# Polysketch attention and ReGLU FFN on one core: the first 512 tokens in feature layout, their queries loaded first, and a new order of all operations

## The chip, the core and the metric

The kernel runs on one core of one Trainium2 chip. The engines are written as in the profile: PE (TensorE; PEld is its weight load), DVE (VectorE), ACT (ScalarE), POOL (GpSimd) and SP (SyncE, which here issues transfers). The metric is the device time of one execution in microseconds (us), the median of several runs. The clock column of the profile is the share of the full TensorE clock that was granted.

## The reference, cut to what matters

```python
# q, k, v: (4 batches, 4 heads, 1088 tokens, 32), float32; S1, S2: (8, 32)
def phi(x):
    a = np.einsum('rd,bhsd->bhsr', S1, x)
    b = np.einsum('rd,bhsd->bhsr', S2, x)
    return np.einsum('bhsi,bhsj->bhsij', a, b).reshape(*x.shape[:-1], r * r)
q_p, k_p = (phi(q), phi(k))
kv = np.einsum('bhsf,bhsd->bhfd', k_p, v)
z = np.sum(k_p, axis=2)
num = np.einsum('bhsf,bhfd->bhsd', q_p, kv)
den = np.einsum('bhsf,bhf->bhs', q_p, z)[..., None] + 1e-06
x = num / den                       # laid out as 4352 tokens x 128
# w_gate, w_val: (128, 1536); w_out: (1536, 128)
gate = np.maximum(x @ w_gate, 0.0)
out = (gate * (x @ w_val)) @ w_out  # (4352, 128), float32
```

So each token's query and key are sketched twice to 8 numbers, the outer product gives 64 features, the keys of a batch are summed into a state of 64 x 32 (and a normaliser z of 64) for each head, every query is multiplied with its batch's state and divided by the normaliser, and the result goes through an FFN with a gate. No token needs another's result except through the states, so the FFN of a batch's tokens can run as soon as the keys of this batch, and these queries, are through.

## The kernel before

A `Plan` holds every operation (`Op`) with its engine and what it comes after. `START` gives each operation a rank; `Plan.run` sorts by rank and emits in that order, which is thus the order of each engine's queue. An engine takes its queue in order: an operation that waits holds up all behind it. `BANKS` gives each `Lease` its PSUM bank, and `WARM` says ahead of which operations dummy matmuls on a tile of zeros stand (L967). `POOL_UNITS` lists the FFN units whose product of gate and value is made by POOL.

The operations come in four families.

- `K(b)`, keys and values of batch b: transposes of the loaded keys on DVE (`kt1`, L467 and L471), the sketch on PE (`ksk`, L486, in runs of 8 x 32 columns for four groups of partitions, with the ninth tile of every group in matmuls of 32 columns of its own, half of them on a weight of zeros `wz`), a transpose back on DVE (`kt2`, L491), the normaliser (`z`, `zc`, then `w`, `wc`), the outer products (`kphi`, POOL or DVE, L527), casts of v to f16 on ACT (`vc`, and `vcr`, L548, for the ninth tile, which has loads of its own), the state on PE (`kv`, L554) and its copy into a block-diagonal tile `bd` (`kve`; L564 on ACT for batch 0, L566 on DVE for the others).
- `First`, the first two tiles (256 tokens) of batch 0, on a short way of their own: sketch (L630), transposes, the normaliser by `aT` and `csk` (L642, L648), then on DVE `f bw` (L654), `f red` (L610), `f rd` (L612); numerators on PE (`f num`, L677) with tokens on partitions; `f xd` (DVE, L615) multiplies by the reciprocal; a PE transpose (`f xr`, L684) and an ACT copy (`f x`, L621) give x with features on partitions, as the FFN wants it.
- `Q(b, ...)`, all other queries: `qt1` (DVE, L940), sketch `qsk` (PE, L748, L755), `qt2` (DVE, L761), `bw` (POOL, L769), `red` and `rd` (DVE, L775, L779), `an` and `qphi` (POOL, L783, L789), a transpose `qtr` (for the first tiles on PE, L804, else a DMA from the SP queue, L796), `num` (L816) and a copy `x` to the FFN's input (ACT, L829). `Q(0)` takes tiles 2 to 7 of batch 0, in parts of two and four.
- `F(u, group, ...)`, 102 FFN units of 512 columns of gate and of value: `g` and `v` (PE, L870), `relu` (ACT, L875), `h` (DVE, L883) or, for POOL's units, `vcp` (ACT, L879) and `hp` (POOL, L887), then `o` (PE, L894), which adds up over the units of a group in one PSUM bank; at its last unit `oe` (ACT, L902) and the stores. Groups are (0,0,2), (0,2,2), (0,4,4) for batch 0 as batch, first tile, number of tiles; two of four tiles for each later batch; and a last one of 256 tokens, the ninth tiles of all batches.

The loads: batch 0's keys, S1, S2, a first 256 columns of q (`q00`, 128 KB), half of v, and then the rest of q (`q01`, 416 KB) on SP; the other half of v and all nine weight blocks as casting transfers from POOL's queue. q has four buffers, k and v two each.

Of the kernel before, what the change touches and what calls it, by code (L numbers as in the profile page):

```python
# [9 lines left out]
FP32 = mybir.dt.float32  # L10
FP16 = mybir.dt.float16
# [12 lines left out]
POOL_UNITS = set(range(20, 96, 6))  # L24
START = [
# [48 lines left out]
]  # L74
BANKS = [
# [22 lines left out]
]  # L98
WARM = {33: 29, 62: 1, 64: 3, 152: 1, 66: 1, 79: 6, 80: 3, 81: 3, 83: 2, 158: 2, 266: 10}
# [39 lines left out]
def kernel(  # L139
# [53 lines left out]
    q_sb = [sb([128, NC * D], FP32, f"q_sb{b}") for b in range(B)]  # L193
    v32 = [sb([128, H, NX * D], FP32, f"v32_{b}") for b in range(2)]
    v32 = v32 + v32
    vr32 = sb([64, B, H, D], FP32, "vr32")
# [5 lines left out]
    kT = [sb([128, NC * 32], FP32, f"kT{b}") for b in range(2)]  # L202
# [5 lines left out]
    id16 = sb([2 * R, 2 * R], FP32, "id16")  # L208
# [4 lines left out]
    maskp = sb([128, 2], FP32, "maskp")  # L213
    maskh = sb([128, 4], FP32, "maskh")
    wS = sb([128, 2, 2, R], FP32, "wS")
    wz = sb([128, 32], FP32, "wz")
# [18 lines left out]

    def by_q(t, lo, hi):
        return t[:, lo // 2 * QY:hi // 2 * QY].rearrange("p (y a c) -> p a y c", a=4, c=64)

    def load_v0(eng, y, a):
        eng.dma_start(  # L240
            out=v32[0][32 * a:32 * a + 32, :, y * GX * D:(y + 1) * GX * D],
# [763 lines left out]
```

## Time and profile before

| what | value |
|---|---|
| runs | 105.74, 106.45, 107.58 us; median 106.45 |
| span of the profiled execution | 105.4 us |
| busy PE, DVE, ACT, POOL | 94.6, 84.8, 78.4, 62.5 us |
| instructions | 3159 |
| dummy matmuls (L967) | 61, 7.2 us |
| transferred | 11.87 MB |

The span of the profiled execution runs from its first instruction to its last; it lies 0.3 us under the fastest run and 1.05 under the median. A row of a group gives busy time, mean time of one in ns, and the idle time ahead of them with what ended it; a row of the chain gives start, length and what; a row of stretches gives the borders, the length, each engine's busy time, the granted clock, the share of the transfer engines and GB/s.

### The profile page before, as it was taken

Reading aid. Unit: us, or ns where it says so; the run is one execution under the profiler, and the core shown is the slowest. Engines: PE = TensorE matmul, PEld = TensorE weight load, DVE = VectorE, ACT = ScalarE, POOL = GpSimd, SP = SyncE. Lnnn points to the kernel's source line nnn. Section 1 sums busy time; section 2 is a strip of 40 time slices with the busy share of each in tenths; the row PEclk is TensorE's granted clock in tenths of the full one; section 3 lists DMA queues with packets and bytes.
Section 4 is the critical chain, followed back from the end, with each engine's and each line's share of the span. In section 5 each row is a group of like instructions: output and inputs, shape, how many; then the busy total and the mean of one; then the engine's idle time right before and its main releaser. Section 6 shows DMA issues by size and latency. Waiting matters only on the chain.

```text
span 105.4 us, 3159 instructions
## 1 busy us (share of the span) xinstructions
PE 94.6 (90%) x1239; PEld 65.9 (63%) x1239; DVE 84.8 (80%) x184; ACT 78.4 (74%) x160; POOL 62.5 (59%) x75
## 2 busy tenths in 40 slices
PE   6997249999999999999999989999999999999930
PEld 6777127578577666656665555667666666779910
DVE  4595297289999999999999978998997794978820
ACT  5207212769899779989979899897598999995820
POOL 6989129769238354999898499787540724404000
PEclk9999975599999999999999999999999999999995
DMA  2999999996000795700057610005293021221442
GB/s 57 272 183 285 279 277 256 221 236 165 8 0 3 142 301 146 176 9 0 0 99 231 126 61 0 6 0 109 50 126 102 24 48 51 42 101 62 100 96 57
DMA packets 15311, 11.87 MB, mean 113 GB/s; under 512 B 9408, under 2 KB 13376, under 8 KB 15296
## 3 DMA queue, kind: packets, MB, share of 16 engines
q1 hardware_dynamic: 13184, 10.04, 38.7%
q0 software_dynamic: 1872, 1.31, 8.5%
q10 hardware_dynamic: 240, 0.33, 1.1%
q8 instruction: 9, 0.15, 0.6%
q14 instruction: 6, 0.05, 0.2%
HBM read 9.05 MB, written 2.23 MB: 107 GB/s over the span
## 4 chain that ended last, share of the span: by engine, by line
PE 67%; DMA 11%; DVE 5%; SPq 4%; ACT 3%; issue 3%; POOL 2%; DVEq 0%
PE ps L870 38%; PE ps L894 18%; DMA q_sb<-in_q_dram 7%; DMA qpt<-qqp 5%; DVE ht L883 4%; PE ps L816 2%; PE ps L748 2%; POOL qqp L789 2%; PE ps L486 2%; SPq L240 2%; ACT g_sb L875 2%; PE ps L967 1%; PE ps L554 1%; SPq L258 1%; PE ps L512 1%
## 5 line engine op out<-in xcount | busy, mean ns | idle before, releaser
L875 ACT ACTIVATE g_sb<-ps 128x512 f16<-128x512 f32 x102 | 55.8, 610 | 7.5 <-PE ps L870 6.8
L883 DVE TENSOR_TENSOR ht<-g_sb,ps 128x512 f16<-128x512 f16 x89 | 56.7, 676 | 5.3 <-PE ps L870 2.9
L894 PE MATMUL ps<-wo,ht 128*128 128x128 f16 x408 | 36.4, 219 | 0.4 <-DVE ht L883 0.4
L894 PEld LDWEIGHTS <-ht 128*128 128x128 f16 x408 | 29.2, 98 | 11.6 <-DVE ht L883 0.8
L870 PE MATMUL ps<-xT,wv 128*128 128x512 f16 (+1 forms) x120 | 36.0, 353 | 0.0
L870 PE MATMUL ps<-xT,wg 128*128 128x512 f16 (+1 forms) x120 | 35.4, 362 | 0.0
L887 POOL TENSOR_TENSOR ht<-g_sb,v_sb 128x512 f16<-128x512 f16 x13 | 15.0, 1156 | 12.2 <-ACT v_sb L879 8.8
L527 POOL TENSOR_TENSOR kp<-kab 128x512 f16<-128x512 f32 (+2 forms) x14 | 15.6, 1136 | 4.7 <-DVE kab L491 4.7
L870 PEld LDWEIGHTS <-wg 128*128 128x128 f16 x120 | 13.1, 117 | 5.3 <-issue 1.4
L789 POOL TENSOR_TENSOR qqp<-qan,qabc 128x1024 f16<-128x1024 f32 (+1 forms) x9 | 15.8, 1758 | 0.7
L870 PEld LDWEIGHTS <-wv 128*128 128x128 f16 x120 | 12.5, 114 | 3.4 <-issue 0.6
L769 POOL TENSOR_TENSOR bw<-qabc 128x128 f32<-128x128 f32 (+1 forms) x9 | 3.8, 428 | 11.4 <-DVE qabc L761 11.3
L967 PE MATMUL ps<-zero 128*128 128x128 f16 x61 | 7.2, 279 | 1.4 <-DVE maskh L309 1.0
L879 ACT CAST v_sb<-ps 128x512 f16<-128x512 f32 x13 | 7.8, 603 | 0.1
L940 DVE STREAM_TRANSPOSE qT<-q_sb 128x544 f32<-128x544 f32 (+2 forms) x9 | 5.7, 659 | 2.7 <-DMA q_sb<-in_q_dram 2.7
L902 ACT ACTIVATE o_sb<-ps 128x512 f32<-128x512 f32 (+1 forms) x10 | 5.4, 542 | 2.4 <-PE ps L894 2.4
L967 PEld LDWEIGHTS <-zero 128*128 128x128 f16 x61 | 5.6, 130 | 2.0 <-DVE maskh L309 1.0
L829 ACT CAST xT<-ps 128x512 f16<-128x512 f32 (+1 forms) x9 | 4.9, 543 | 2.6 <-PE ps L816 2.6
L761 DVE STREAM_TRANSPOSE qabc<-ps 128x512 f32<-128x512 f32 (+2 forms) x12 | 5.7, 517 | 1.0 <-PE ps L755 0.5
L783 POOL TENSOR_TENSOR qan<-qabc,qrd 128x128 f32<-128x128 f32 (+1 forms) x9 | 3.5, 384 | 4.0 <-DVE qrd L779 3.9
L554 PEld LDWEIGHTS <-kp 128*128 128x128 f16 x72 | 4.1, 98 | 2.1 <-issue 0.7
L554 PE MATMUL ps<-v,kp 128*128 128x64 f16 x72 | 4.8, 193 | 0.6 <-ACT v L545 0.6
(91 smaller groups left out, 74.3 us busy)
## 6 DMA issues: line engine op xcount, KB each, us to landing
k_sb<-in_k_dram SPq DMA_DIRECT2D x3, 544.0 KB, 8.7
q_sb<-in_q_dram SPq DMA_DIRECT2D x3, 544.0 KB, 3.7
v<-in_v_dram SPq DMA_DIRECT2D x12, 128.0 KB, 5.7
out_dram<-o_sb SPq DMA_DIRECT2D x4, 256.0 KB
out_dram<-o_sb SPq DMA_DIRECT2D x4, 128.0 KB
out_dram<-o_sb SPq DMA_DIRECT2D x8, 64.0 KB, 1.6
q_sb<-in_q_dram SPq DMA_DIRECT2D x1, 416.0 KB, 7.1
wg<-in_moe_w_gate_dram POOLq DMA_DIRECT2D x3, 128.0 KB, 6.0
```

The source lines that it names most:

```text
L527: eng.tensor_tensor(out=self.kp[:, lo:hi].rearrange("p x g (i a c) -> p (x g i) a c", i=2, a=R), in0=a[:, :, :, None].to_broadcast([128, n ...
L554: nc.tensor.matmul(m[:, 64 * p:64 * p + 64], self.kp[:, x, p], v16[self.b][:, 2 * p:2 * p + 2, x * D:(x + 1) * D], start=(x == 0 and p == ...
L761: nc.vector.transpose(self.abc[:, lo:lo + m, 2 * i2:2 * i2 + 2].rearrange("p x h f -> p h x f"), pair(ls[i2])[:, :, lo * 32:(lo + m) * 32] ...
L789: nc.gpsimd.tensor_tensor(out=self.qp[:, lo:hi].rearrange("p x g (i a c) -> p (x g i) a c", i=2, a=R), in0=self.an[:, lo * H:hi * H, :, No ...
L870: nc.tensor.matmul(bank(l)[:, y * self.W:(y + 1) * self.W], w[:, j // 4, :, j % 4], x, start=True, stop=True, skip_group_check=True)
L875: nc.scalar.activation(out=self.gs, in_=bank(l), func=ACTF.Relu)
L879: nc.scalar.copy(out=self.vs, in_=bank(l))
L883: nc.vector.tensor_tensor(out=self.ht, in0=self.gs, in1=bank(l), op=ALU.mult)
L887: nc.gpsimd.tensor_tensor(out=self.ht, in0=self.gs, in1=self.vs, op=ALU.mult)
L894: nc.tensor.matmul(o[:, s], self.ht[:, y * W + s * 128:y * W + (s + 1) * 128], wo[:, j // 4, j % 4], start=(j == 0 and s == 0), stop=(j == ...
L940: nc.vector.transpose(qT[b][:, lo:hi], q_sb[b][:, lo:hi])
L967: nc.tensor.matmul(PS[:, 7, 0:128], zero, zero, start=True, stop=True, skip_group_check=True)
```

## The change

- `First` takes four tiles (512 tokens) in two halves. The numerators are computed with the state as the weights, so they come out with features on partitions. The reciprocal is spread over 32 columns of each head (`f rx`, DVE), transposed on PE in f32 with `id32` (`f rT`), copied by ACT (`f rTe`), and `f xd` multiplies straight into the FFN's input. `f xr` and `f x` are gone. `Q(0)` takes tiles 4 to 7 only, in two parts of two.
- q00 is 512 columns (256 KB), q01 the rest (288 KB). q has three buffers; batch 3 takes that of batch 0.
- Keys and values are in runs of 9, 9, 8, 8 tiles for the four groups of partitions, so `ksk` of a later batch is eight matmuls of 288 columns, the ninth tile has no loads, casts or zero weight of its own, and `z` and `kv` use 64 partitions for it.
- `kve` is one DVE operation with a mask for every batch.
- v's second half of batch 0 is loaded by SP as f32 and cast by ACT. wo0, wg1 and wv1 are loaded by SP as f32 into free `qabc` buffers and cast by ACT (`cw`); wg0, wv0, wo1, wg2, wv2, wo2 stay on POOL, in new places: wv0 stands behind both `bw` of Q(0).
- POOL's units are 15 (five of the first 22) where they were 13 (one of the first 22). There are 36 dummies for 61.
- The groups of batch 0 are four of two tiles. The last unit's product and `o` come in two halves, its eviction is split over ACT and DVE, with one store each on ACT and SP. All other groups have four stores each on SP.
- All of `START`, `BANKS` and `WARM` is new. SP's loads stand in the order s1, s2, k01, q00, eight of v, wo0, q01, wg1, wv1, k1, q1, k2.

In the queues of the new program the stretch around the first tile reads: DVE `f bw 0`, `f red 0`, `f bw 1`, `f rd 0`, `f rx 0`, `qt1 0 4`, `f red 1`, `kve 0`, `f rd 1`, `f rx 1`, four `qt2`, `red`, `f xd 0`, `rd`, `red`, `rd`, `kt1 1 0`, `f xd 1`, `kt1 1 1`; PE `kv 0 8`, `f tr 0`, six dummies, `qsk 0,4`, `f rT 0`, `f num 1`, `f num 0`, `f rT 1`, then `g 2`, `g 0`, `g 1`, `v 2`, `g 3`, `g 9`, `v 3`, `g 7`, a `qtr` of Q(0), `ksk 1`, `g 6`, `num` and the second `qtr` of Q(0), `z 1`, `v 21`, `v 0`. Here `g 2`, `v 2`, `g 3`, `v 3`, `g 9` and `v 21` use the blocks wg1 and wv1, `g 0`, `g 1`, `g 6`, `g 7` use wg0, and `v 0` uses wv0.

The core of the diff:

```diff
-POOL_UNITS = set(range(20, 96, 6))
+POOL_UNITS = [2, 12, 14, 20, 21, 34, 41, 45, 46, 58, 65, 66, 80, 81, 97]
+WL = {'g0': 'POOL', 'v0': 'POOL', 'o0': 'SP', 'g1': 'SP', 'v1': 'SP', 'o1': 'POOL', 'g2': 'POOL', 'v2': 'POOL', 'o2': 'POOL'}
...
-WARM = {33: 29, 62: 1, 64: 3, 152: 1, 66: 1, 79: 6, 80: 3, 81: 3, 83: 2, 158: 2, 266: 10}
+WARM = {34: 15, 153: 4, 67: 11, 173: 6}
...
+    KRUN = [(0, KX), (KX, KX), (2 * KX, NX), (2 * KX + NX, NX)]
+    KHALF = [[(4 * a, 4) for a in range(4)], [(16, 5), (21, 5), (26, 4), (30, 4)]]
...
-    lq0 = [P.add("SP", f"ld q0{y}", part(q_sb[0], q, y * QY, QY if y == 0 else NC * D))
-           for y in range(2)]
+    lq0 = [P.add("SP", "ld q00", part(q_sb[0], q, 0, 2 * QY)),
+           P.add("SP", "ld q01", part(q_sb[0], q, 2 * QY, NC * D))]
...
+        raw = q_abc[i].rearrange("p x h f -> p (x h f)")[:, e * 512:(e + 1) * 512]
+        ld = P.add(eng, f"ld w{kind}{t}",
+                   lambda: {"SP": nc.sync, "ACT": nc.scalar}[eng].dma_start(out=raw, in_=src))
+        op = P.add("ACT", f"cw {kind}{t}", lambda: nc.scalar.copy(out=dst, in_=raw), [ld, ftab])
...
+        def sk(self, la, lo, hi, run):
+            m = hi - lo
+            for p in range(2):
+                rows = slice(64 * p, 64 * p + 64)
+                wt = wS[rows].rearrange("p w i r -> p (w i r)")
+                for a in range(4):
+                    c = run[a][0]
+                    nc.tensor.matmul(
+                        bank(la, p)[32 * a:32 * a + 32, lo * 32:hi * 32], wt,
+                        self.kT[rows, c * 32:(c + m) * 32], start=True, stop=True,
+                        skip_group_check=True)
...
+            nc.vector.tensor_tensor(
+                out=bd[self.b], in0=bank(lm)[:, 0:128].rearrange("f (p g d) -> f p g d", p=2, g=2),
+                in1=maskg[:, None, :, None].to_broadcast([128, 2, 2, D]), op=ALU.mult)
...
-            xd = P.add("DVE", "f xd", lambda: nc.vector.tensor_tensor(
-                out=self.xt.rearrange("p x (h d) -> p (x h) d", d=D),
-                in0=bank(ln)[:, 0:n * 128].rearrange("p (y d) -> p y d", d=D),
-                in1=self.rd[:, :, None].to_broadcast([128, n * H, D]), op=ALU.mult),
-                [num, o3], drop=[ln])
-            xr = P.add("PE", "f xr", lambda: self.xr(lx), [xd, fident], take=[lx])
-            self.x_op = P.add("ACT", "f x", lambda: nc.scalar.copy(
-                out=xT[:, 0:n * 128], in_=bank(lx).bitcast(FP16)[:, 0:n * 128]), [xr],
-                drop=[lx])
...
+                rx = P.add(RXE, f"f rx {y}", lambda h=h, y=y: cp[RXE](
+                    out=self.rx[:, 2 * y:2 * y + 2].rearrange("p x h d -> p (x h) d"),
+                    in_=self.rd[:, h, None].to_broadcast([128, 2 * H, D])), [o3])
+                rt = P.add("PE", f"f rT {y}", lambda y=y, l=lr: self.rt(l, y), [rx, fid32],
+                           take=[lr])
+                rts.append(P.add("ACT", f"f rTe {y}", lambda y=y, l=lr: nc.scalar.copy(
+                    out=self.rT[:, 256 * y:256 * y + 256], in_=bank(l)[:, 0:256]), [rt],
+                    drop=[lr]))
...
+        def num(self, ln, x):
+            for p in range(2):
+                nc.tensor.matmul(
+                    bank(ln)[64 * p:64 * p + 64, 0:256],
+                    bd[0][:, p].rearrange("f g d -> f (g d)"), self.pt[:, x, p],
+                    start=True, stop=True, skip_group_check=True)
...
+        def xd(self, ln, y):
+            t = slice(256 * y, 256 * y + 256)
+            nc.vector.tensor_tensor(out=xT[:, t], in0=bank(ln)[:, 0:256], in1=self.rT[:, t],
+                                    op=ALU.mult)
...
-    groups = [(0, 0, 2), (0, 2, 2), (0, 4, 4)]
+    groups = [(0, 0, 2), (0, 2, 2), (0, 4, 2), (0, 6, 2)]
...
-    qs = [Q(0, 2, [(0, 2), (2, 4)], 0, [ks[0]], [t0b, t0r], [], True)]
+    qs = [Q(0, GX, [(0, 2), (2, 2)], 0, [ks[0]], [t0r], [], True)]
```

More of the change, by code (lines that the diff above doesn't have):

```diff
@@ L23 @@
 NH = 12
-POOL_UNITS = set(range(20, 96, 6))
-START = [
[48 rows of a table removed]
+POOL_UNITS = [2, 12, 14, 20, 21, 34, 41, 45, 46, 58, 65, 66, 80, 81, 97]
+KBC = [(2, 4), (4, 8)]
+WL = {'g0': 'POOL', 'v0': 'POOL', 'o0': 'SP', 'g1': 'SP', 'v1': 'SP', 'o1': 'POOL', 'g2': 'POOL', 'v2': 'POOL', 'o2': 'POOL'}
+V0L = [['SP', 'SP', 'SP', 'SP'], ['SP', 'SP', 'SP', 'SP']]
+FILL = 'DVE'
+RXE = 'DVE'
+RINGS = [['ld s1', 'ld s2', 'ld k01', 'ld q00', 'ld v000', 'ld v001', 'ld v002', 'ld v003', 'ld v010', 'ld v011', 'ld v012', 'ld v013', 'ld wo0', 'ld q01', 'ld wg1', 'ld wv1', 'ld k1'], ['ld wg0', 'ld wv0', 'ld wo1', 'ld wg2', 'ld wv2', 'ld wo2'], ['vc 0 0', 'gate'], ['zero', 'masks']]
+START = [
[44 rows of a table added]
 ]
 BANKS = [
[22 rows of a table removed]
[19 rows of a table added]
 ]
-WARM = {33: 29, 62: 1, 64: 3, 152: 1, 66: 1, 79: 6, 80: 3, 81: 3, 83: 2, 158: 2, 266: 10}
+WARM = {34: 15, 153: 4, 67: 11, 173: 6}
 class Lease:
@@ L302 @@
-    lwo = [P.add("POOL", f"ld wo{t}", lambda t=t: nc.gpsimd.dma_start(
-        out=wo[:, t].rearrange("p j m -> p (j m)"),
-        in_=moe_w_out[t * 512:(t + 1) * 512].rearrange("(p j) m -> p (j m)", j=4)), [fident])
-        for t in range(3)]
-    def fill1():
-        nc.vector.memset(maskp, 0.0)
-        nc.vector.memset(maskh, 0.0)
+    ftab = P.add("ACT", "table", table, [f0])
+    fid32 = P.add("POOL", "id32", lambda: make_identity(nc, id32))
+    fident = P.add("ACT", "ident", lambda: nc.scalar.copy(out=ident, in_=id32), [fid32, ftab])
@@ L447, in __init__ @@
                       for h in range(2)]
-            vc.append(P.add("ACT", f"vcr {b}", self.vcr, lvr0 if b == 0 else lvr))
             vcs[b] = vc
@@ L452, in __init__ @@
                 for l in lv[b + 2][:4]:
[L453 removed]
+                    l.after += vc if b or V0L[1][0] != "POOL" else vc[:1]
             lm = Lease(P)
@@ L578 @@
     q_rd = qtile("qrd", [128, NX * H], FP32)
+    cp = {"ACT": nc.scalar.copy, "DVE": nc.vector.tensor_copy, "POOL": nc.gpsimd.tensor_copy}
     class First:
         def __init__(self, kk, qt1):
-            self.kk, n = kk, 2
-            self.n, self.col = n, 0
+            self.kk, n = kk, 4
+            self.n = n
             self.ab = sb([128, 2, n, 2, 16], FP32, "fab")
             self.aT = sb([128, n * 128], FP32, "faT")
-            self.bw = sb([128, n * H, R + 1], FP32, "fbw")
+            self.bw = fbw
@@ L605, in __init__ @@
-            at = P.add("PE", "f aT", lambda: self.at(lat), [qt1, s1r_op], take=[lat])
-            ate = P.add("ACT", "f aTe", lambda: nc.scalar.copy(
-                out=self.aT, in_=bank(lat)[:, 0:n * 128]), [at], drop=[lat])
-            cs = P.add("PE", "f csk", lambda: self.csk(lc), [kk.zc_op, ate], take=[lc])
-            o1 = P.add("DVE", "f bw", lambda: self.mul(lc), [t2, cs, fe], drop=[lc])
-            o2 = P.add("DVE", "f red", lambda: nc.vector.tensor_reduce(
-                out=self.dn, in_=self.bw, axis=AX.X, op=ALU.add), [o1])
@@ new lines, in __init__ @@
+            self.x_ops = []
+            for y in range(2):
+                x = slice(2 * y, 2 * y + 2)
+                lt, ln = Lease(P), Lease(P)
+                phi = P.add("POOL", f"f phi {y}", lambda x=x: self.phi(x), [t2])
+                tr = P.add("PE", f"f tr {y}", lambda x=x, lt=lt: self.tr(lt, x), [phi, fident],
+                           take=[lt])
+                pt = P.add("ACT", f"f pt {y}", lambda x=x, lt=lt: nc.scalar.copy(
+                    out=self.pt[:, x].rearrange("f x g t -> f (x g t)"),
+                    in_=bank(lt).bitcast(FP16)[:, 0:512]), [tr], drop=[lt])
+                num = P.add("PE", f"f num {y}", lambda x=x, ln=ln: self.num(ln, x),
+                            [pt, kk.kve], take=[ln])
+                self.x_ops.append(P.add(
+                    "DVE", f"f xd {y}", lambda y=y, ln=ln: self.xd(ln, y), [num, rts[y]], drop=[ln]))
@@ L659, in phi, with rt @@
-        def phi(self):
-            n = self.n * H
-            src = self.ab.rearrange("p w x g (i r) -> p w (x g i) r", r=R)
+                out=self.bw[:, 2 * H * y:2 * H * y + 2 * H, 0:R],
+                in0=self.ab[:, 1, 2 * y:2 * y + 2].rearrange("p x g (i r) -> p (x g i) r", r=R),
+                in1=bank(lc)[:, 0:64].rearrange("p (x r) -> p x r", r=R), op=ALU.mult)
+        def rt(self, lr, y):
+            for e in range(2):
+                nc.tensor.matmul(
+                    bank(lr)[:, e * 128:(e + 1) * 128],
+                    self.rx[:, 2 * y + e].rearrange("p h d -> p (h d)"), id32, start=True,
+                    stop=True, skip_group_check=True)
@@ L668, in tr @@
             o = bank(lt).bitcast(FP16).rearrange("f (x g t) -> f x g t", g=2, t=128)
-            for x in range(self.n):
+            for e in range(2):
                 for p in range(2):
-                    nc.tensor.transpose(o[:, x, p], self.qp[:, x, p], ident)
-        def num(self, ln):
-            for x in range(self.n):
-                for p in range(2):
-                    c0 = x * 128 + p * 64
-                    nc.tensor.matmul(bank(ln)[:, c0:c0 + 64], self.pt[:, x, p],
-                                     bd[0][:, p].rearrange("f g d -> f (g d)"),
-                                     start=True, stop=True, skip_group_check=True)
@@ L681, in xr @@
-        def xr(self, lx):
-            o = bank(lx).bitcast(FP16)
-            for x in range(self.n):
-                nc.tensor.transpose(o[:, x * 128:(x + 1) * 128], self.xt[:, x], ident)
+                    nc.tensor.transpose(o[:, e, p], self.qp[:, x.start + e, p], ident)
+        def num(self, ln, x):
+            for p in range(2):
+                nc.tensor.matmul(
+                    bank(ln)[64 * p:64 * p + 64, 0:256],
+                    bd[0][:, p].rearrange("f g d -> f (g d)"), self.pt[:, x, p],
+                    start=True, stop=True, skip_group_check=True)
@@ L706, in __init__ @@
                                  lambda i2=i2, lo=lo, m=m: self.t2(ls, i2, lo, m),
-                                 [s] + old, drop=[ls[i2]]) for i2 in range(2)]
+                                 [s] + old + staged[i], drop=[ls[i2]]) for i2 in range(2)]
             for lo, m in parts:
@@ L856, in __init__ @@
-            self.o_op, self.h_op = o, h
-            if self.last:
-                ev = P.add("ACT", f"oe {u} {n}", self.oe, [o], drop=[self.lo])
-                if grp[0] is not None:
-                    parts = n // 2 if grp[0] == 0 else 4 if grp[0] == B - 1 else 1
-                    for y in range(parts):
-                        P.add("SP", f"st {u}", lambda y=y: self.st(y), [ev])
-                else:
-                    P.add("SP", f"st {u} r", lambda: self.str(nc.sync, 0), [ev])
-                    P.add("ACT", f"st {u} r", lambda: self.str(nc.scalar, 1), [ev])
+                hs = [P.add("POOL", f"hp {u}", self.hp, [a, a2])]
+            elif self.last and grp[0] is None:
+                cols = [(0, 2), (2, 2)]
+                hs = []
+                for c, _ in cols:
+                    hs.append(P.add("DVE", f"h {u} {c}", lambda c=c: self.h(lv_, 128 * c, 256),
+                                    [a, vv] + hs, drop=[lv_]))
+            else:
+                hs = [P.add("DVE", f"h {u}", lambda: self.h(lv_, 0, 512), [a, vv], drop=[lv_])]
@@ new lines, in __init__ @@
+            pre = [prev.o_op] if not self.first else []
+            for i, (h, (c, m)) in enumerate(zip(hs, cols)):
+                o = P.add("PE", f"o {u} {n}" + (f" {c}" if len(cols) > 1 else ""),
+                          lambda c=c, m=m: self.o(c, m), [h, lwo[t]] + pre,
+                          take=[self.lo] if self.first and i == 0 else [])
+                pre = [o]
+            self.o_op = o
+            if self.last and grp[0] is None:
+                self.os = sb([128, 2 * DM], FP32, "o_last")
+                for e in range(2):
+                    ev = P.add(["ACT", "DVE"][e], f"oe {u} e{e}", lambda e=e: self.oer(e), [o],
+                               drop=[self.lo])
+                    P.add(["ACT", "SP"][e], f"st {u} r{e}",
+                          lambda e=e: self.str([nc.scalar, nc.sync][e], e), [ev])
+            elif self.last:
+                ev = P.add("ACT", f"oe {u} {n}", self.oe, [o], drop=[self.lo])
+                for a in range(4):
+                    P.add("SP", f"st {u} {a}", lambda a=a: self.st(a), [ev])
```

353 lines of the change are left out of this document (173 added, 180 removed), and 133 rows, old and new, of tables (BANKS, START).

## The prediction

> **What bounds the kernel now.** I read the page first, then busy time in six stretches cut at the marks of the chain, then the chain at the start.
>
> ```profile
> span 105.4 us, 3159 instructions
> ...
> PE 94.6 (90%) x1239; PEld 65.9 (63%) x1239; DVE 84.8 (80%) x184; ACT 78.4 (74%) x160; POOL 62.5 (59%) x75
> ```
>
> ```profile
> 0.00:12.40 12.40, 9.44 (x173) 8.05 (x173) 6.74 (x32) 4.72 (x14) 9.95 (x21) 1.00 0.94 212
> 12.40:16.60 4.20, 2.00 (x44) 1.50 (x45) 3.93 (x13) 0.37 (x1) 1.38 (x4) 0.76 1.14 272
> 16.60:21.40 4.80, 4.80 (x52) 2.98 (x50) 1.80 (x5) 2.77 (x5) 3.97 (x5) 0.50 1.11 233
> 21.40:25.00 3.60, 3.36 (x46) 2.77 (x47) 3.40 (x6) 2.77 (x6) 2.73 (x4) 1.00 1.08 232
> 25.00:60.00 35.00, 34.59 (x457) 22.92 (x456) 34.43 (x68) 31.62 (x65) 24.09 (x25) 1.00 0.39 97
> 60.00:100.00 40.00, 39.44 (x465) 27.09 (x463) 33.79 (x62) 35.45 (x70) 20.40 (x21) 1.00 0.27 59
> ```
>
> The columns of a stretch are length, PE, PEld, DVE, ACT and POOL busy, granted clock, DMA share, GB/s. From 25 to 60 us PE and DVE are both full (0.41 and 0.57 us idle of 35); from 60 to 100 PE alone is (0.56 idle of 40). So there is nothing to gain after 25 us except by taking work off PE, and in the middle off DVE too. The slack lies ahead: until 16.6 us PE waits for the first tile, and from 16.6 to 21.4 it is busy but at half clock, so that 4.80 us hold 2.40 us of full-speed work. DVE is idle for 3.0 us there.
>
> ```profile
> 5.30 7.11 DMA q_sb<-in_q_dram
> ...
> 14.28 0.44 DVE fxt L615
> ...
> 15.61 1.22 PE ps L967 x10
> 16.84 3.41 PE ps L870 x16
> ```
>
> ```profile
> PE ps L748 <- DVE fbw L654: 2.4, 1, 2.4
> ```
>
> Start, length, and what (the second fence is from the waits): the second part of q, issued at 5.30, lands at 12.41; behind it on DVE stand two transposes, then the normaliser of the first tile, then fxt, the PE transpose, the ACT copy, ten dummy matmuls at half clock, and only then the FFN's gate and val matmuls. They follow 16.84 - 12.41 = 4.43 us behind the landing. The row of the waits is PE's longest stop: 2.4 us ahead of the query sketch.
>
> ```profile
> 14.00:15.00 1.00, 0.54 (x33) 0.24 (x3) 0.87 (x4) 0.00 (x0) 0.00 (x0) 0.78 1.12 304
> 15.00:16.00 1.00, 0.54 (x7) 0.39 (x5) 0.96 (x5) 0.37 (x1) 0.79 (x2) 0.50 1.18 247
> ...
> 20.00:21.00 1.00, 1.00 (x18) 0.45 (x24) 0.00 (x0) 0.81 (x3) 1.00 (x1) 0.50 0.94 247
> 21.00:22.00 1.00, 1.00 (x32) 0.80 (x16) 0.40 (x1) 0.60 (x2) 0.59 (x1) 0.81 1.17 239
> ```
>
> The clock column (0.78, 0.50 ... 0.50, 0.81) puts the half clock from 15 - 0.22/0.50 = 14.56 us to 21 + 0.19/0.50 = 21.38 us: 6.8 us, behind the stop of 2.4.
>
> **The change, part by part.**
>
> *1. When q's second part lands.* The trace's queues over the first 15 us:
>
> ```profile
> q1 hardware_dynamic: 2040, 2.21, 48.6%
> q0 software_dynamic: 1385, 0.88, 41.9%
> ...
> ```
>
> The loads of the whole span, with the median time from issue to landing last:
>
> ```profile
> wg<-in_moe_w_gate_dram POOLq DMA_DIRECT2D x3, 128.0 KB, 6.0
> wv<-in_moe_w_val_dram POOLq DMA_DIRECT2D x3, 128.0 KB, 7.0
> wo<-in_moe_w_out_dram POOLq DMA_DIRECT2D x3, 128.0 KB, 8.2
> ...
> v<-in_v_dram POOLq DMA_DIRECT2D x4, 32.0 KB, 3.6
> ```
>
> Packets, MB, share of the engines' 15 us in the first fence: a MB costs 7.29/2.21 = 3.3 us on the hardware queue, 6.29/0.88 = 7.1 us on the software queue (counted as f16 there). Ahead of the landing before stand, on the software queue, the second half of batch 0's v (128 KB) and four weight blocks (512 KB): 640 KB, 4.6 us; on the hardware queues k (544), q (544), half of v (256) and S: 1352 KB, 4.5 us; in all 9.1. After, the software queue carries wg0 alone (128 KB, 0.9 us), since wv0 and the rest are issued behind the two bw products on POOL; the hardware queues take the other half of v (256) and wo0 as f32 (256) on top: 1864 KB, 6.2 us; in all 7.1. The difference is 2.0 us; I take 1.8, landing at 10.6. From below it is 128 KB that q01 itself is smaller, 0.4 us; from above 2.5, if the order packs better than its sum. DMA: Bandwidth & Descriptors of the Trainium skill (Issuing engine by pattern) says that the hardware path is generally faster than the software path; these two rows agree, for f16 bytes, by 2.2 times.
>
> *2. From that landing to the first gate matmul.* q01 still gates: on DVE its transpose stands ahead of red 1, kve 0, rd 1, rx 1 and four qt2, which all stand ahead of red and xd 0; PE's order has qsk of q01 ahead of the first rT and num. The price by rows:
>
> ```profile
> L940 DVE STREAM_TRANSPOSE qT<-q_sb 128x576 f32<-128x576 f32 x1 | 0.8, 778 | 2.7 <-DMA q_sb<-in_q_dram 2.7
> ...
> L761 DVE STREAM_TRANSPOSE qabc<-ps 128x128 f32<-128x128 f32 x4 | 1.1, 301 | 0.5 <-PE ps L755 0.5
> ...
> L615 DVE TENSOR_TENSOR fxt<-ps,frd 128x256 f16<-128x256 f32 x1 | 0.4, 425 | 0.1
> ...
> L610 DVE TENSOR_REDUCE fdn<-fbw 128x8 f32<-128x72 f32 x1 | 0.2, 228 | 0.0
> ...
> L612 DVE RECIPROCAL frd<-fdn 128x8 f32<-128x8 f32 x1 | 0.2, 204 | 0.0
> ...
> L654 DVE TENSOR_TENSOR fbw<-fab,ps 128x64 f32<-128x64 f32 x1 | 0.2, 184 | 0.0
> ```
>
> 0.78 (transpose) + 0.23 (red) + 0.27 (kve, 128x128, between the 0.18 of 128x64 and the 0.43 of 128x256) + 0.20 (rd) + 0.42 (rx, by L615's size) + 4 x 0.30 (qt2) + 0.23 (red) + 0.42 (xd) = 3.75, with a little issue 3.9. No PE transpose, ACT copy or dummy follows: xd writes x transposed. So 3.9 against 4.43, and the first gate matmul at 14.5 instead of 16.8: 2.3 us earlier (bounds: 0.9 with the lower landing, 3.0 with the upper). The normaliser in feature layout (rT, rTe) stays under those DVE operations unless the clock is half; then four transposes of 290 to 580 ns can cost up to 1 us more, which I leave in the range.
>
> *3. The clock.* Before, 2.4 us are lost after 16.6. The stop ahead of qsk remains in the new order (q01 still comes last), so I expect throttling again, but most of it ahead of the tile: 3.4 us of it behind 14.5 lose 1.7 us. Gain 0.7; bounds: -1.0 (the same 6.8 us, all behind 14.5, lose 3.4) to +2.4 (none). TensorE: Matmul & The Clock Gate (Part 1: The HAM clock gate) of the Trainium skill has a free-running window of some 3.4 us, half rate after an idle one. The trace's 6.8 us is two of them, and the phase can't be read ahead of a run.
>
> *4. DVE's and ACT's load behind the tile.*
>
> ```profile
> L883 DVE TENSOR_TENSOR ht<-g_sb,ps 128x512 f16<-128x512 f16 x89 | 56.7, 676 | 5.3 <-PE ps L870 2.9 <-ACT g_sb L875 1.7
> ...
> L879 ACT CAST v_sb<-ps 128x512 f16<-128x512 f32 x13 | 7.8, 603 | 0.1
> ...
> L887 POOL TENSOR_TENSOR ht<-g_sb,v_sb 128x512 f16<-128x512 f16 x13 | 15.0, 1156 | 12.2 <-ACT v_sb L879 8.8 <-ACT g_sb L875 3.4
> ...
> L548 ACT CAST v<-vr 64x128 f16<-64x128 f32 x4 | 1.2, 294 | 0.7 <-DMA vr<-in_v_dram 0.7
> ```
>
> Of the first 22 units one was POOL's (20), now five are (2, 12, 14, 20, 21): 4 x 0.68 = 2.7 us off DVE, 4 x 0.60 = 2.4 onto ACT, 4.6 onto POOL. With the 3.0 us that DVE idled from 16.6 to 21.4, DVE can follow a start 2.3 + 0.7 = 3.0 earlier. ACT from 12.4 to 25 is busy 5.9 of 12.6 us, and three casts of staged weights (0.6 each) and 2.4 of vcp fit, though not where each is due. Behind the first 22 units ten go to POOL where twelve did, so DVE gets 2 x 0.68 = 1.4 us back; from 60 us on it has 6.2 us idle to cover that, so I cost it at nothing (1.4 if it fell between 25 and 60, where DVE is full).
>
> *5. Keys' sketch, batches 1 to 3.*
>
> ```profile
> 20.25 1.14 PE ps L486 x32
> ...
> 40.54 0.69 PE ps L486 x25
> ```
>
> ```profile
> L486 PE MATMUL ps<-kT,wS 64*32 64x128 f32 x32 | 0.9, 281 | 0.3 <-DVE wS L351 0.3
> ```
>
> Sixteen records of 288 columns take the place of 32 (16 of 256 and 16 of 32; the second row lacks some of its records). The whole took 0.69 at full clock, so 16 cost 0.35 if records decide and 0.69 if columns do. I take 0.45, so 0.24 less for each of three batches: 0.7 (0 to 1.0). The four vcr casts (0.29) go as well, off ACT.
>
> *6. The end.*
>
> ```profile
> 100.24 0.70 DVE ht L883
> ...
> 100.98 0.41 PE ps L894 x4
> ...
> 101.42 0.38 ACT o_sb L902
> ```
>
> ```profile
> 102.19 0.81 SPq L922 DMA_DIRECT2D out_dram<-o_sb  x2
> ```
>
> Two h halves overlap with two matmuls, half the eviction on each of two engines, and one store a queue: 0.2 off the matmuls, 0.1 off the eviction, 0.4 off the second issue. But SP has more stores to issue ahead of it (0.4 each); I take 0.4 (0 to 0.7).
>
> *7. What it adds as waits.* wv0 is issued on POOL behind both bw, which need qt2: 10.6 + 0.9 + 0.7 + 4 x 0.3 + two bw of 0.32 gives about 14.1. It lands 3.6 (the small blocks of v) to 7.0 us later (the wv row above), 17.7 to 21.1. PE's order has seven gate and three val operations, ksk, two qtr, num and z ahead of v 0: two records of 0.213 at half clock (row 16.84) make 0.215 an operation at full, so 10 x 0.215 + 1.3 = 3.45 us of full-speed work. With 3.4 us at half clock behind 14.5 that is done at 14.5 + 3.4 + (3.45 - 1.7) = 19.7. So PE stops 0 to 1.4 us; I take 0.5, for a landing at 20.2 by the wg row. Behind v 0 on PE stand v 6, the keys' w of batch 1, and its qsk. Secondly k1's landing: behind q01 come wg1, wv1 (256 KB each) and k1 (544): 1056 KB x 3.3 = 3.5 us, 14.1, and kt1 of it stands on DVE ahead of xd 1; then k2 the same way ahead of zc of batch 1. These cost 0 if on time and 0.7 each if a fifth of the queue goes to others: 0.7. The casts and vcp that come out of turn on ACT, 0.5. In all 1.7 (0 to 4).
>
> *Sum*: 2.3 + 0.7 + 0.7 + 0.4 - 1.7 = 2.4 us. The profiled execution's span is 105.4, the median of the runs 106.45, 1.05 above, which I keep: 105.4 - 2.4 + 1.05 = 104.05, given as 104.1.
>
> **The rivals.**
>
> *A, the clock stays whole*: part 3 gives +2.4 instead of +0.7, so 102.4. PE is then at v 0 at 14.5 + 3.45 = 17.95, so it holds only if wv0 takes no more than some 4 us; at 6.0 the gain is lost there again. For it: q01 comes 1.8 sooner, so PE's stop of 2.4 shrinks, and wv0 is alone on its queue. Against: 36 dummies are left of 61, fewer to fill the gap.
>
> *B, the early start is eaten*: q01 comes only by its own size sooner (0.4, so 0.9 in part 2), because v's second half and wo0 now stand ahead of it on its own queue. The sum is 0.9 + 0.7 + 0.7 + 0.4 - 1.7 = 1.0 and, if DVE (34.43 of 35) lets none of the clock's 0.7 through, 0.3: 106.1. In this case the change doesn't do what it is laid out for.
>
> *C, slower*: wv0 late at the head of PE's queue. If its landing takes 8.2 us, as the wo row has it, and it is issued at 14.1, it lands at 22.3 and PE stands for 2.6 us ahead of v 0.
>
> Before, a stop of 2.4 was followed by 6.8 us at half clock, 3.4 us lost, now in the FFN itself: the sum is 2.4 - (2.6 - 0.5) - 3.4 = -3.1, so 109.5. It decides from a landing about 2 us behind v 0's place, near 21.7; for it: the wo row; against: three rows (wg, wv, v) are shorter, and the queue has only wv0 on it then.
>
> **How the numbers follow.** My forecast has 0.42, A 0.15, B 0.24, C 0.19. The bound of 2%, about what a measurement of this kernel can tell from no change, lies at 104.3 and 108.6. The forecast's own spread of some 1 us puts two thirds of it, 0.28, below 104.3; with A 0.43 faster. The remaining 0.14, B's 0.24 and 0.02 of C are within: 0.40. Slower: 0.17. The range: 102.0 takes in most of A, 108.0 all of B and the bounds of part 7 up to its upper half; the most of C is left out.
>
> **What would show it.** Right: q's second part landing at 10 to 11 us; the first gate matmul at 14 to 15; no dummies between xd 0 and it; the h's of units 2, 12, 14 on POOL; PE's wait for wv under 1 us; at the end one store a queue, the last issue near 100. Wrong: q01 landing after 11.8 (B); PE waiting over 2 us for wv, or k's transposes waiting on DVE over 1 us each (C); the clock at 1.00 from 14 to 20 (A); PE not full between 25 and 60, which would say that DVE or ACT has become the bound.

## The result: 10% slower, and the profile after

The changed kernel took 116.2 us (median of 4 runs, 115.5 to 121.8) against 106.4 before: a ratio of 1.099, with a 95% interval of 1.088 to 1.111. The forecast was 104.1, the range 102 to 108. Single runs of one kernel lie up to some 6% apart, and every ratio here compares the fast runs of one kernel with the fast runs of the other.

The page and the stretches of the changed kernel, cut at the same marks as before (length, PE, PEld, DVE, ACT, POOL busy, clock, DMA share, GB/s):

```profile
span 113.8 us, 3085 instructions
...
PE 100.6 (88%) x1188; PEld 71.7 (63%) x1188; DVE 85.2 (75%) x190; ACT 82.5 (72%) x165; POOL 60.3 (53%) x71
```

```profile
12.40:16.60 4.20, 4.20 (x40) 3.83 (x39) 2.57 (x10) 1.90 (x5) 0.00 (x0) 1.00 0.85 279
16.60:21.40 4.80, 4.69 (x59) 3.44 (x59) 3.35 (x12) 3.67 (x9) 2.71 (x6) 1.00 1.06 257
21.40:25.00 3.60, 3.20 (x52) 1.78 (x50) 3.52 (x7) 3.08 (x8) 3.47 (x6) 1.00 0.98 176
25.00:60.00 35.00, 30.43 (x397) 22.18 (x398) 29.08 (x56) 27.89 (x57) 27.19 (x28) 1.00 0.44 112
60.00:100.00 40.00, 38.48 (x424) 24.66 (x423) 30.87 (x57) 34.46 (x67) 20.24 (x21) 1.00 0.25 42
```

Two things stand out. From 25 to 60 us PE is idle for 4.6 of 35 us where it was 0.4, and DVE for 5.9 where it was 0.6: no engine is full, so they wait for each other. And from 12.4 to 16.6 PE is busy without a gap where it was idle for over half of the time, and the tile still is not ready: the first gate matmul starts at 19.6 us, 3.0 later than before (16.6). Below stands the group of all gate matmuls with the times of its first and last start, before and after.

```profile
L870 PE MATMUL ps<-xT,wg x120: 270/379/417, 16.6 to 97.9; 128*128 128x512 f16 x84, 128*128 128x256 f16 x36
```

```profile
L901 PE MATMUL ps<-xT,wg x132: 269/376/382, 19.6 to 106.1; 128*128 128x512 f16 x72, 128*128 128x256 f16 x60
```

What PE, ACT and DVE wait for (engine, line, releaser: us in total, times, longest):

```profile
PE ps L901 <- DVE qabc L779: 4.3, 7, 0.9
...
ACT g_sb L906 <- DVE qabc L779: 2.5, 3, 1.2
...
DVE qabc L779 <- PE ps L901: 1.7, 2, 0.9
```

An evacuation is the instruction that takes a result out of its PSUM bank; here it transposes on the way and reads a pair of banks at once. Gate and value matmuls wait for transposing evacuations of query sketches, relus wait for them, and they in turn for gate and value matmuls. By the data none of these needs the other. Before, PE's longest waits had no such row. The first place, batch 1's queries, in order of time:

```profile
26.88 0.73 PE L766 MATMUL ps<-qT,wq 32*32 32x256 f32 x32
...
27.54 0.41 PE L901 MATMUL ps<-xT,wg 128*128 128x256 f16 x2
...
27.78 0.38 PE L901 MATMUL ps<-xT,wv 128*128 128x256 f16 x2
...
28.05 0.72 DVE L779 STREAM_TRANSPOSE qabc<-ps 128x512 f32<-128x512 f32 x1
28.81 0.60 ACT L906 ACTIVATE g_sb<-ps 128x512 f16<-128x512 f32 x1 [1.16 <-DVE qabc L779]
28.83 0.38 PE L901 MATMUL ps<-xT,wg 128*128 128x256 f16 x2 [0.66 <-DVE qabc L779]
...
29.04 0.38 PE L901 MATMUL ps<-xT,wv 128*128 128x256 f16 x2
...
29.53 0.72 DVE L779 STREAM_TRANSPOSE qabc<-ps 128x512 f32<-128x512 f32 x1 [0.76 <-PE ps L901]
...
30.30 0.38 PE L901 MATMUL ps<-xT,wg 128*128 128x256 f16 x2 [0.88 <-DVE qabc L779]
```

The sketch's 32 matmuls (26.88) go to two pairs of banks, (2, 6) and (1, 7); one DVE instruction evacuates a pair. The program as built has these waits: the first evacuation waits for `g 12`, which writes bank 3; the relu of unit 12, which reads bank 3, waits for the evacuation, and so does `g 13`, which writes bank 5. The second, of banks 1 and 7, waits for `v 1`, which writes bank 4, and for the relu that reads bank 3; `g 15` then waits for it. All of these banks lie between the two of the pair. So in this program an instruction that reads two banks with a stride is ordered against everything in the banks between. These are semaphore waits of the built program; the data doesn't ask for them, and no run shows whether the chip would. Before the change all 16 pairs in BANKS are neighbours; after it 11 of 16 are not. The experiments test this.

### The profile page after: what moved, and what is told of

Same layout as the page of the kernel before. It is cut to its first block, busy times and chain, and to the rows that moved or that the text cites. A ratio compares the mean times of both kernels' runs of the same rounds, so it can differ in the third digit from the quotient of the medians.

```text
span 113.8 us, 3085 instructions
## 1 busy us (share of the span) xinstructions
PE 100.6 (88%) x1188; PEld 71.7 (63%) x1188; DVE 85.2 (75%) x190; ACT 82.5 (72%) x165; POOL 60.3 (53%) x71
## 4 chain that ended last, share of the span: by engine, by line
PE 75%; DVE 13%; ACT 3%; DMA 2%; issue 2%; SPq 0%; DVEq 0%
PE ps L901 37%; PE ps L929 20%; DVE qabc L779 4%; PE ps L556 3%; PE ps L489 3%; DVE kT L480 2%; DVE ht L916 2%; DVE kab L495 2%; PE ps L1004 2%; DMA s<-in_S_dram 2%; PE ps L652 2%; PE ps L503 2%; ACT g_sb L906 2%; PE ps L660 1%; PE ps L834 1%
## 5 line engine op out<-in xcount | busy, mean ns | idle before, releaser
L916 DVE TENSOR_TENSOR ht<-g_sb,ps 128x512 f16<-128x512 f16 (+1 forms) x88 | 55.3, 670 | 8.6 <-PE ps L901 7.0
L901 PE MATMUL ps<-xT,wg 128*128 128x512 f16 (+1 forms) x132 | 33.2, 331 | 3.9 <-DVE qabc L779 3.7
L929 PEld LDWEIGHTS <-ht 128*128 128x128 f16 x408 | 27.9, 98 | 13.1 <-issue 3.4
L929 PE MATMUL ps<-wo,ht 128*128 128x128 f16 x408 | 34.9, 219 | 0.9 <-DVE kab L495 0.9
L901 PE MATMUL ps<-xT,wv 128*128 128x512 f16 (+1 forms) x132 | 34.3, 331 | 1.5 <-DVE qabc L779 0.6
L921 POOL TENSOR_TENSOR ht<-g_sb,v_sb 128x512 f16<-128x512 f16 x15 | 17.2, 1156 | 19.0 <-ACT v_sb L910 12.9
L531 POOL TENSOR_TENSOR kp<-kab 128x512 f16<-128x512 f32 (+2 forms) x14 | 15.8, 1134 | 1.6 <-DVE kab L495 1.5
L787 POOL TENSOR_TENSOR bw<-qabc 128x128 f32<-128x128 f32 (+1 forms) x9 | 3.6, 409 | 15.2 <-DVE qabc L779 15.1
L779 DVE STREAM_TRANSPOSE qabc<-ps 128x128 f32<-128x128 f32 (+1 forms) x12 | 5.7, 503 | 5.2 <-PE ps L901 1.7
L1004 PE MATMUL ps<-zero 128*128 128x128 f16 x36 | 4.6, 311 | 1.0 <-DVE zero L284 1.0
L556 PEld LDWEIGHTS <-kp 128*128 128x128 f16 (+1 forms) x72 | 4.3, 108 | 1.3
L556 PE MATMUL ps<-v,kp 128*128 128x64 f16 (+1 forms) x72 | 5.0, 205 | 0.0
L1004 PEld LDWEIGHTS <-zero 128*128 128x128 f16 x36 | 3.8, 145 | 1.5 <-DVE zero L284 1.0
```

Source lines behind the costliest of these rows:

```text
L531: eng.tensor_tensor(out=self.kp[:, lo:hi].rearrange("p x g (i a c) -> p (x g i) a c", i=2, a=R), in0=a[:, :, :, None].to_broadcast([128, n ...
L556: nc.tensor.matmul(m[:, 64 * p:64 * p + 64], self.kp[k, x, p], v16[self.b][k, 2 * p:2 * p + 2, x * D:(x + 1) * D], start=(x == 0 and p == ...
L779: nc.vector.transpose(self.abc[:, lo:lo + m, 2 * i2:2 * i2 + 2].rearrange("p x h f -> p h x f"), pair(ls[i2])[:, :, lo * 32:(lo + m) * 32] ...
L901: nc.tensor.matmul(bank(l)[:, y * self.W:(y + 1) * self.W], w[:, j // 4, :, j % 4], x, start=True, stop=True, skip_group_check=True)
L916: nc.vector.tensor_tensor(out=self.ht[:, t], in0=self.gs[:, t], in1=bank(l)[:, t], op=ALU.mult)
L921: nc.gpsimd.tensor_tensor(out=self.ht, in0=self.gs, in1=self.vs, op=ALU.mult)
```

## The experiments

**Theory 1, the clock at the start, with 29 dummies again.** The chain of the changed kernel has PE from 4.9 to 19 us, at rates like these:

```profile
10.74 1.17 PE ps L1004 x11
...
12.29 1.71 PE ps L660 x8
```

A dummy takes 0.106 us here. The clock column says 1.00, but in runs where the clock is whole by then the same 11 dummies take 0.61. The column shows nothing ahead of the first recorded change.

```diff
-WARM = {34: 15, 153: 4, 67: 11, 173: 6}
+WARM = {34: 29, 153: 4, 67: 11, 173: 6}
```

> The changed kernel with 29 dummy matmuls ahead of the first matmul, as before the change, in place of 15. Theory 1 (the 15 dummies end at 2.6 us, PE then waits for S until 3.7 and never reaches full clock ahead of the tile; all matmuls from 3.7 to 19 us run at half speed, and the late start puts the queues out of step): dummies run to 4.1 us, the 11 dummies ahead of the z work go by at 56 ns instead of 107, the first gate matmul comes by 16.5 us instead of 19.6, and PE is dense from 25 us on: 103 to 107 us. Theory 2 (the new order itself makes PE wait for banks and DVE for PE): the first gate matmul comes 2 to 3 us earlier, but some 5 us of stops on PE between 20 and 70 us stay: 111 to 114 us. Theory 3 (the half clock has nothing to do with it, the transfers set the start): within 1 us of 116.2.

Measured: 117.2 us, ratio 1.088 (1.064 to 1.112), no better than the change. In the profiled run the first gate matmul did come at 16.1 us. But then PE stood. The chain, the stretches and PE's wait in this run:

```profile
15.83 9.76 DMA wv<-in_moe_w_val_dram
```

```profile
20.00:25.00 5.00, 1.26 (x24) 0.74 (x22) 2.20 (x5) 2.82 (x6) 4.37 (x6) 1.00 1.11 199
25.00:30.00 5.00, 4.15 (x46) 2.07 (x47) 2.58 (x5) 0.87 (x2) 0.32 (x1) 0.50 0.74 238
30.00:35.00 5.00, 3.89 (x28) 1.81 (x28) 2.37 (x5) 2.25 (x4) 2.85 (x4) 0.50 0.04 15
```

```profile
PE ps L901 <- DMA wv<-in_moe_w_val_dram: 3.5, 1, 3.5
```

wv0, issued at 15.83, landed 9.76 us later, PE stood 3.5 us at `v 0`, and the clock was half from 25 to 35. This is rival C of the prediction, place and consequence, in one execution: the profiled run took 118.7 us, the shortest two 114.2 and 115.8, and how long PE stood in those isn't known. In the changed kernel itself wv0 was issued at 18.7 and landed at 25.5, and PE waited only 0.6 us, because it was so late itself.

**The kernel before with 15 dummies.**

```diff
-WARM = {33: 29, 62: 1, ...
+WARM = {33: 15, 62: 1, ...
```

> The kernel before the change with 15 dummy matmuls ahead of the first matmul in place of 29. Theory 1: the sketches of the keys and the normaliser run at half speed here too, and the first gate matmul comes later than 16.6 us. But its way to the first tile is shorter and waits for q until 12.4 us anyway: 107 to 110 us. Theory 2: the old order takes a late start better, 106 to 108 us. Theory 3: 106.4 us, no change.

Measured: 105.7 us, ratio 0.996 (0.990 to 1.002). The old start does not need them: its dummies were slow until 9.3 us here, but the first gate matmul still came at 15.2. The likely reason is that it has less work for PE ahead of the tile (3.2 us busy of the 5 from 10 to 15, where the changed kernel has 5.0). So the dummies taken out are not the cause by themselves.

**Theory 4, far banks, in the changed kernel.** Each evacuation of a pair that is not neighbouring becomes two instructions of one bank:

```diff
+            if far(ls[i2]):
+                for i in range(2):
+                    nc.vector.transpose(
+                        self.abc[:, lo:lo + m, 2 * i2 + i],
+                        bank(ls[i2], i)[:, lo * 32:(lo + m) * 32].rearrange("p (x f) -> p x f", f=32))
+                return
             nc.vector.transpose(
                 self.abc[:, lo:lo + m, 2 * i2:2 * i2 + 2].rearrange("p x h f -> p h x f"),
                 pair(ls[i2])[:, :, lo * 32:(lo + m) * 32].rearrange("p h (x f) -> p h x f", f=32))
```

and likewise for the keys and in `First`.

> The changed kernel, where each transposing evacuation of two banks that do not lie side by side (11 of its 16 pairs of banks) is two instructions of one bank each; nothing else is changed. Theory 4 (such an instruction reads with a stride from bank to bank, and in the built program it waits for the matmuls and relus of all banks between the two, and they for it: 4.1 us of PE, 2.5 of ACT and 1.7 of DVE waits in the profile): PE's waits for the qabc transposes go, DVE has some 11 instructions of 0.1 us fixed cost more, the start is as late as before (first gate matmul 19.5 us): 110 to 113 us. Rival (the stops are order and load of DVE, not banks): 116 to 118 us.

Measured: 110.2 us, ratio 1.030 (1.014 to 1.046). (The 4.1 us of PE in the expectation are 4.3 by the waits above.) No matmul on PE waits for qabc or kab any more, and PE is full again from 25 us on:

```profile
25.00:60.00 35.00, 34.21 (x459) 24.78 (x457) 32.35 (x71) 30.95 (x63) 31.34 (x32) 1.00 0.50 120
60.00:100.00 40.00, 39.99 (x436) 26.49 (x434) 33.18 (x63) 36.29 (x72) 17.33 (x18) 1.00 0.24 47
```

**Theory 4 in the kernel before.** Only the names of the banks are changed, so that its order, instructions and sharing stay and 11 pairs are torn apart:

```diff
-BANKS = [ (0,), (1,), (2, 3), (4, 5), (3,), ...
+BANKS = [ (0,), (5,), (1,3), (4,6), (3,), ...      # bank i -> (0, 5, 1, 3, 4, 6, 2, 7)[i]
```

> The kernel before the change with its eight PSUM banks renamed (0 5 1 3 4 6 2 7 in place of 0 to 7) everywhere; order, instructions and sharing of banks are the same, but 11 of its 16 pairs, none before, have banks that are not neighbours. Theory 4: waits of PE and ACT for the transposing evacuations appear, 108 to 113 us. Rival (which banks make a pair does not matter): 106.4 us, within 1 us.

Measured: 112.9 us, ratio 1.063 (1.049 to 1.077); all four runs (112.07 to 114.32) lie above all twelve of the kernel before on the same chip (105.62 to 110.32). Waits of the changed kernel's kind appear in a kernel that had none:

```profile
PE ps L867 <- DVE kab L488: 2.0, 2, 1.1
...
PE ps L867 <- DVE qabc L758: 1.5, 2, 0.9
PE ps L891 <- DVE qabc L758: 1.3, 1, 1.3
```

So theory 4 is shown from both sides: 6 to 7% of the 10.

**What the rest is.** With the dummies and with wv0 right behind wg0 (one rank of START, 107 to 25), banks as changed:

> The changed kernel with 29 dummies at the start, and with wv0 issued right behind wg0 on POOL. Theory 5 (the late landing of wv0 took what the whole clock had brought: PE stood for 3.5 us at v 0, then half clock): first gate matmul about 16.5 us, no wait for wv, and 109 to 112 us, since the waits at the far banks are still there. Rival (only the banks matter): 115 to 117 us.

Measured: 115.0 us, 1.084 (1.074 to 1.094): the banks alone are enough to hold it there; in the profiled run the first gate matmul was at 19.2 in spite of 29 dummies. All three cures together:

> All three in one: 29 dummies, wv0 behind wg0, pairs of far banks in two instructions. If the three causes (half clock at the start, late wv0, false waits between banks) are the whole loss and the change is otherwise worth what the prediction summed without its waits (4.1 us): 101 to 105 us. If something else of the new order holds it back: 106 to 110 us.

Measured: 107.05 us, 1.0075 (0.999 to 1.016), first gate matmul at 15.6 in the profiled run and PE's only long stop behind it 1.3 us. So the three cures take the loss away to within this interval, but the 4.1 us of gain do not appear: by the expectation's second branch something else of the new order holds it back. Each of the two small cures beside the divided transposes:

> Divided transposes and 29 dummies, wv0 late as in the change. If the half clock at the start is what is left of the loss behind the banks (3.0 of 116.2 against before 106.4): 107 to 108.5 us. If the late wv0 takes it back, as it did with the far banks: 109.5 to 111.

> Divided transposes and wv0 behind wg0, 15 dummies as in the change. If each cure is worth something alone: 108 to 109.5 us. If wv0 only matters once the start is early (first gate matmul at 20 us, wv0 needed at 25): 110 us, as with the divided transposes alone.

Measured: 109.3 us, 1.030 (1.021 to 1.040), and 108.8 us (106.6 to 110.1, no ratio). The dummies alone bring nothing beside 1.030, wv0 alone is not told apart from nothing; both together bring some 2%, with intervals that just touch. In the profiled run with the dummies the first gate matmul came at 20.3 all the same (20.0 with wv0 alone), so the early start that they were to bring isn't in it, and whether a late wv0 would take it back is not shown.

**Neighbouring banks instead of divided instructions.** BANKS handed out anew with all pairs adjacent, in four steps of cures:

> The changed kernel with its PSUM banks handed out anew so that all 16 pairs are neighbours, as before the change; order and instructions are the same, no transpose is divided. Theory 4 (waits between far banks): as the divided version or a little better, since DVE has no instructions more: 108 to 110.5 us. Rival (the division helped in another way, by shorter DVE instructions): 113 us or more.

> Neighbouring banks and 29 dummies, wv0 still behind both bw. If the late wv0 costs what it did with the far banks (3.5 us of PE waiting, then half clock): 108 to 111 us, no better than without the dummies. If wv0 lands in time once the rest runs: 105 to 107 us.

> Neighbouring banks, 29 dummies, wv0 behind wg0. Sum of the three causes: 103.5 to 106.5 us, 0.5 to 1 less than with divided transposes (107.05), whose 11 further DVE instructions are gone. If the clock throttles again behind the wait for the keys of batch 1, at its upper end.

> As a_near_all, with 16 more dummies ahead of the z matmuls of batch 1, where PE stood 1.3 us and the clock was then half for some 3.4 us. If a filled wait keeps the clock whole: 1 to 2 us less than a_near_all, 102 to 105 us. If the dummies do not count or fall behind the wait: the same or 0.9 us more.

Measured: 110.3 (1.042, 1.020 to 1.064), 110.4 (1.045, 1.029 to 1.061), 109.0 (1.032, 1.020 to 1.044), 110.9 (1.026, 1.014 to 1.038). The first agrees with the divided version within the intervals, so it is the banks and not the shorter instructions. The second came out as expected for a late wv0, for which PE waited 2.0 us in the profiled run. The third missed: the dummies write bank 7, which the new map also gives to operations ahead of them, and in the profiled run one group waited for such an evacuation.

```profile
PE ps L1009 <- DVE kab L500: 0.8, 1, 0.8
```

The fourth is a miss too: more dummies at a later wait gave nothing; its profiled run was at half clock from 10 to 15 us, far ahead of them. With bank 7 kept free until the last dummy, then dummies fitted to the waits at the start (24 and 6 for 29), then wg2 and wv2 issued earlier:

> As a_near_all, with the banks handed out so that bank 7, into which the dummies write, belongs to no operation until the last dummy has gone (in a_near_all two groups of dummies waited for a transposing evacuation, 0.8 us, and the clock fell at 7 to 11 us). If that was the difference to a_all3: 104.5 to 107 us, a little under a_all3 (107.05) since 11 DVE instructions are gone. If not: 108 to 109 us.

> As a_near7_all, with 24 dummies at the start and 6 ahead of the first sketch of keys, so that they do not run past the landing of S (3.6 us) and fill PE's wait behind it. a_near7_all ran between 104.4 and 110.5 us; if that spread is whether the clock is whole by 5 us, the upper runs go: median 104 to 106.5. If not: 107 to 109 us again.

> As a_near7_fill, with wg2 and wv2 issued behind the first f phi on POOL, where PE waited for them (1.0 us between 25 and 30 us in a_near7_all). If that wait is what is left: 1 us less than a_near7_fill. If the loads of batch 2's keys come later for it: the same or more.

Measured: 107.9 us (104.35 to 110.5, no ratio); 109.2 (ratio 1.000, 0.984 to 1.016); 107.6 (ratio 0.997, 0.981 to 1.013). Each of these two ratios rests on two of the six runs; by the median of all runs they stand at 109.2 and 107.6, where the kernel before has 107.6 in the same round. So the repaired change is level with the kernel before in its best executions, and no version was shown to be better. The spread stays. In the best profiled run of these three (105.5 us, the first kernel) the chain has

```profile
10.32 0.61 PE ps L1009 x11
...
15.21 0.42 DVE xT L706
```

and the first gate matmul follows at 15.7. In that of the second kernel (110.2 us) the same 11 dummies take 1.17 us in place of 0.61, and that matmul comes at 20.0.

What is left behind the banks goes with the start. Of the eleven profiled versions of the change without false waits at far banks, three had their first gate matmul at 15.6 to 16.7 us and took 105.5 to 107.1; eight had it at 19.3 to 20.3 and took 108.3 to 112.1.

Why the same start becomes early in one execution and late in another can be narrowed down from the clock changes that the kept traces record. In all 17 profiles they lie on a grid of 3.41 us, and where the grid lies against the start differs from execution to execution. In the twelve profiles with 24 or 29 dummies at the start, the clock was first whole at 3.6 to 4.8 us where a point of the grid fell between 0.2 and 1.4 us (six), and at 8.9 us or later where it fell between 1.6 and 2.9 (six). An early rise is not enough: in five of those six the clock fell again at 7.0 to 8.2 us, in three of them until 17.3 or later. What PE must do between two points to raise or keep the clock was not settled, and no experiment moved the grid.

## Why the prediction was wrong, point by point

- **Sum and range.** The step that failed is the one that isn't in the sum. Part 7 listed waits from late loads, and 0.5 us for casts out of turn on ACT; that "all of START, BANKS and WARM is new" was costed by START and WARM. The false waits between far banks cost 6 to 7%, near 7 us. They could have been read ahead: the new list has pairs such as (2, 6) and (1, 7), and the built program's waits name matmuls in the banks between. No row of the old trace could show them, since all its pairs are neighbours, so this was an unknown cost that wanted a bound and got none. The second step that failed is part 2: the first gate matmul came at 19.6 us and not at 14.5. By estimate the two make up nearly all of the 12.1 us between forecast and measurement: 6 to 7 by the experiments on the banks, and 5.1 at the start if a later start counts in full. The sign "PE not full between 25 and 60" did come, but not for the reason given with it, since DVE and ACT weren't full either (29.1 and 27.9 of 35 us).
- **Part 1, q's landing.** 10.6 was forecast; the transfer was issued at 6.98 and took 4.7, so 11.7, 0.7 earlier than before instead of 1.8. It decided nothing. Of the two rivals, B's condition (after 11.8) was just missed.

```profile
q_sb<-in_q_dram SPq DMA_DIRECT2D x1, 288.0 KB, 4.7
```

- **Part 2, the way to the tile.** Wrong. I had DVE's 3.9 us behind q01 as the bound; it was PE. q01's transpose started at 14.6 on DVE, 2.9 after the landing, because `f bw` ahead of it waited for PE's csk (2.3 us). Twice as many tiles in f32 (aT, csk, and rT as an addition) at half speed filled PE from 4.9 to 19.1 us. I left "up to 1 us" for this.

```profile
DVE fbw L666 <- PE ps L660: 2.3, 2, 1.9
```

```profile
14.61 0.77 DVE L977 STREAM_TRANSPOSE qT<-q_sb 128x576 f32<-128x576 f32 x1
```

- **Part 3, the clock.** A throttle was expected between q's wait and the tile, 0.7 us of gain. What came was a clock that didn't rise until 18.9 us, hidden by a column that reads 1.00 until the first change; by the column, rival A's sign (1.00 from 14 to 20) would even count as seen. The rate of the dummies was there to be read in the trace before: 29 of them fill 0.99 to 4.2 us, 0.107 each, and later ones take half. The Trainium skill's page TensorE: Matmul & The Clock Gate (Part 1: The HAM clock gate) says that the idle state is half rate and that some 3.4 us of sustained work release it. The trace agrees with the first, and only partly with the second: among the twelve profiles with 24 or 29 dummies (2.6 to 3.2 us of work) the clock was first whole at 3.6 to 4.8 us in six, at some 9 in three, and at 18.7 to 23.3 in three.
- **Part 4.** DVE's relief is there (five of the first units on POOL), but DVE was busy for only 29.1 of the 35 us from 25 to 60, and no run shows that it was worth anything.
- **Part 5, the sketch.** Mis-sized: 16 records of 288 columns take 0.65 us, not 0.45, so the columns decide and the gain is 0.04 a batch instead of 0.24.

```profile
31.12 0.65 PE ps L489 x16
```

- **Part 6, the end.** Wrong in sign. The two halves of the last eviction lie in one bank and went one behind the other (in the built program DVE's half waits for ACT's semaphore), and two stores of the group before are issued behind the last one on SP. From the last `o` to the last issue it takes 1.95 us (109.38 to 111.33); before 1.61 (101.39 to 103.00).

```profile
109.40 0.28 ACT L945 ACTIVATE o_last<-ps 128x128 f32<-128x128 f32 x1 [0.82 <-PE ps L929]
...
109.71 0.29 DVE L942 TENSOR_SCALAR o_last<-ps 128x128 f32<-128x128 f32 x1 [0.69 <-ACT o_last L945]
...
110.43 0.90 SPq L951 DMA_DIRECT2D out_dram<-o_sb  x2
```

- **Part 7 and rival C.** Right as a mechanism, not as the cause here: issue at 18.7 where 14.1 was forecast, 6.8 us to land, a wait of only 0.6 since PE came later. With the early start restored it took 9.76 us to land and PE 3.5 us, followed by half clock, as rival C has it (2.6 and half clock). C was given a chance of 0.19.

## What to carry to other kernels

In a program built like this one, an access with a stride over PSUM banks can be ordered against everything between its ends, so give such pairs neighbouring banks, or divide the instruction, and look in the built program for waits on banks that the instruction doesn't touch. Two engines that read one bank can be ordered by such waits too, as at the end of this kernel. When a start is shortened on one engine, count the whole work of the others up to that point at the slower of their clocks, and what the earlier arrival needs next (here a weight block), before the gain is written down.

## What had not been expected of the hardware

The clock column reads 1.00 until the first recorded change, though matmuls run at half speed: 0.107 us a dummy at 1 us in both kernels, and 0.056 in the kernel before once the clock has risen. Its changes lie on a grid of 3.41 us whose place differs between executions: three versions with the same order and the same 29 dummies had a whole clock first at 4.5, 18.7 and 23.3 us. A start that is bound by PE then differs by over 4 us in its first gate matmul (15.6 to 20.3). A software weight load of 128 KB took between 3.6 us from issue to landing (wg0, at 5.1, in the changed kernel) and 9.8 us (wv0 at 15.8, in the profiled run with 29 dummies, where loads of k, q and v had been issued shortly ahead of it).
